# Four query heads of the second batch loaded ahead of its second keys and values, and the last batch's first expert layer in eight block products instead of seven

## The chip, the cores and the metric

The kernel runs on one core of one Trainium2 chip. The metric is the device time of one execution in microseconds (us). Three executions of the kernel before took 369.51, 369.53 and 370.15 us, median 369.53 us. A difference of about 0.2% (0.74 us) is the least that a measurement of this kernel can tell from no change.

Five engines work side by side, each on its own queue in order: PE (TensorE, matrix products, with PEld for its weight loads), DVE (VectorE), ACT (ScalarE), POOL (GpSimd) and SP (SyncE, which here only issues transfers). Sixteen DMA engines move data. PE reads from SBUF and writes to PSUM.

## The reference

Attention over sorted blocks, then a mixture of four experts. Sizes: batch 4, 8 heads, 768 positions, head size 64; 8 blocks of 96 positions.

```
P = sort_net                      # (4, 8, 8, 8)
repeat 5 times:
    P = exp(P - max); P = P / rowsum; P = P / colsum
k_sorted[b,h,i] = sum_j P[b,h,i,j] k_block[b,h,j]      # v the same
attn = softmax(q_block k_sorted_block^T / 8)           # 96 x 96, block by block
x = attn v_sorted_block                                # (4*768, 512)
p = domain_probs / sum(domain_probs)                   # (3072, 4)
out = sum_e p[:, e] * (relu(x w1[e]) w2[e])            # w1 512x1024, w2 1024x512
```

All products are computed on PE with 16-bit operands and sums of 32 bits.

## The kernel before, in words

**Batches and chunks.** The expert layers of a batch are done in three chunks of 256 tokens. While PE computes the experts of batch b, the attention of batch b+1 is worked in between: the lists `PLAN0` (for b = 0) and `PLAN` (b = 1, 2) name, for each chunk and each slot in it, which attention step is called there. A slot is a place between groups of matmuls. The order of instructions on each engine is the order in which the Python code issues them. The chunks of batch 0 do expert 0 ahead, in functions of their own.

**Attention steps of a batch.** Per pair of heads `pr` (0 to 3): `st_v` and `st_k` mix the blocks of values and keys on PE, ACT copies the result; `st_q` transposes the queries of the pair by a DMA on SP's queue (tile `qT`); `st_s` makes the scores on PE (line 405) from `kT` and `qT`; `st_a` makes attn times v (line 437), DVE normalises it into `xsl`; `st_x` transposes `xsl` into the expert input `xT` by a DMA on SP's queue. Keys, values and queries come from memory by DMAs on POOL's queue (`load_natural`, line 109, four heads at a time; `load_queries`, line 120, one head at a time; `st_n` loads the two heads of one pair). They lie in slices of one tile, `arena`. Each load on POOL's queue also waits for the eighth load before it to have landed.

**Start of batch 1's attention.** After the last expert weights (27 to 38 us of landing time each) POOL's queue has, in this order: values 0, keys 0, query heads 0 and 1, values 1, keys 1 (the numbers are the halves of the heads), then three additions of the first chunk's output, then query heads 2 and 3, two additions, query heads 4 to 7. Heads 2 and 3 stand in slot 11 of chunk 0 of `PLAN0`, heads 4, 5 and 6, 7 in slots 0 and 4 of chunk 1.

**First expert layer of a chunk, batches 1 and 2** (`chunk_first`): for each of four experts two groups of 16 matmuls, each with 128x128 weights and 256 columns of `xT` (line 742), into a PSUM buffer of two banks (`psM`, two buffers). DVE then takes max with zero times the token's expert weight from PSUM into `Hb` (line 748) and makes sums of `Hb` blocks into `Sb` (`h_sums`, lines 725 to 731). `pb`, the token weights of a chunk, is loaded on SP's queue once the last user of the chunk before it is done.

**Second expert layer, all chunks:** seven block products instead of eight (a two by two block scheme with sums of blocks), each of 16 matmuls of 256 columns (line 777; line 1069 in the last batch), with the sums of `w2` blocks made once on DVE. DVE, ACT and POOL add up the results, SP stores them.

**Last batch before the change** (`last_chunk`, `seven`): the first layer, too, is done in seven block products per expert. The weight sums s1 to s3 lie in `arena`, s4 in place of a block of `w1`; `input_sums` makes these 16 sums on DVE (line 919) during batch 2, by the list `PLAN_A`. `token_sums` makes four sums of `xT` blocks per chunk (line 935). Each product is 8 matmuls with 128x128 weights and 128 columns (line 981), so 56 per expert and chunk. Partial sums are chained in PSUM banks X, Z, Q; ACT and DVE copy and add them (lines 1001, 1008, 1016, 1017, 1025), and the results go into `Hb` by DVE (line 987) and by ACT with POOL (lines 993, 994). `last_banks` takes over the PSUM of the other pools and issues one matmul of 512 columns (line 948) twice. The first matmul of the next chunk's product, and the product p6 of expert 0, stand inside the last product of the chunk before.

Of the kernel before, what the change touches and what calls it, by code (L numbers as in the profile page):

```python
# [9 lines left out]
F32 = mybir.dt.float32  # L10
# [7 lines left out]
def kernel(  # L18
# [38 lines left out]

    openM, openA = [ctx.enter_context(ExitStack()) for _ in range(2)]
    psM = openM.enter_context(tc.tile_pool(name="psM", bufs=2, space=bass.MemoryType.PSUM))
    psA = openA.enter_context(tc.tile_pool(name="psA", bufs=2, space=bass.MemoryType.PSUM, side="right"))  # L60
# [36 lines left out]

    NW = 4 * R * D
    NQ = NPB * R * 2 * D
    arena = const.tile([P, 4 * NW + NQ + 4 * 4 * P + R * 4 * VW], F16, name="arena")  # L100

# [3 lines left out]
    def load_natural(b, nm, qd):  # L105
        src = {"k": k, "v": v}[nm]
        t = arena[:, ds(("k", "v").index(nm) * 2 * NW + qd * NW, NW)].rearrange("p (h r d) -> p h r d", h=4, r=R)
        natural[(b, nm, qd)] = t
        nc.gpsimd.dma_start(
            t.rearrange("p h r d -> p h (r d)"),  # L110
            src[b, ds(4 * qd, 4)].rearrange("h (p r) d -> p h (r d)", r=R),
        )

    def load_queries(b, heads=range(H)):

        if (b, "q") not in natural:
            natural[(b, "q")] = arena[:, ds(4 * NW, NQ)].rearrange("p (n t h d) -> p n t h d", n=NPB, t=R, h=2)
        t = natural[(b, "q")]
        for h in heads:
            nc.gpsimd.dma_start(t[:, h // 2, :, h % 2, :], q[b, h].rearrange("(t p) d -> p t d", p=P))  # L120
# [64 lines left out]
    kTs, ETs, vs0s, wide = [], [], [], []  # L185
# [4 lines left out]
    for n in range(4):  # L190
        ET = const.tile([P, S + 32], F16, name=f"ET_{n}")
        nc.gpsimd.memset(ET[0:BLK, ds(S, 32)], 0.0)
        ETs.append(ET[0:BLK])
        wide.append(ET)
# [4 lines left out]
    vo = arena[:, ds(4 * NW + NQ + 4 * 4 * P, R * 4 * VW)].rearrange("p (r h w) -> p r h w", r=R, h=4)  # L199
# [122 lines left out]
    def build_PI(eng, n, which):  # L322
        r4 = Rs[:, ds(4 * n, 4), :]
        if which == "k":
            PIk[n] = arena[:, ds(4 * NW + NQ + n % 2 * 4 * P, 4 * P)].rearrange("p (g i c) -> p g i c", g=4, i=NB)
# [6 lines left out]
        else:  # L332
            PIv[n] = arena[:, ds(4 * NW + NQ + (2 + n % 2) * 4 * P, 4 * P)].rearrange("p (g c i) -> p g c i", g=4, i=NB)
# [15 lines left out]
    def st_v(b, pr):  # L349
# [13 lines left out]
        if pr % 2:  # L363
            qd = pr // 2
            vs = att.tile([P, NB, 4, VW], F16, name=f"vs_{b}_{qd}", tag="vs")[0:BLK]
# [63 lines left out]
    def st_a(b, pr):  # L429
        xsl = att.tile([P, NB, 2, D], F16, name=f"xsl_{b}_{pr}", tag="xsl")[0:BLK]  # L430
# [109 lines left out]
    def h_a(qd, qq, ps=None):  # L540
# [11 lines left out]
        if qq not in xsls0:  # L552
            xsls0[qq] = att.tile([P, 2, 4, 2, D], F16, name=f"xsl0_{qq}", tag="xsl")[0:BLK]
# [38 lines left out]
    def stage(b, f, pr):  # L592
# [20 lines left out]
        (0, 9, st_v, 0), (0, 10, st_q, 0), (0, 10, st_v, 1), (0, 11, st_k, 0), (0, 11, st_n, 1), (1, 0, st_q, 1),  # L613
        (1, 0, st_s, 0), (1, 0, st_n, 2), (1, 1, st_k, 1), (1, 1, st_v, 2), (1, 2, st_v, 3), (1, 3, st_q, 2),
        (1, 4, st_s, 1), (1, 4, st_n, 3), (1, 5, st_a, 0), (1, 6, st_x, 0), (1, 7, st_k, 2), (1, 7, st_lv, 0),
# [141 lines left out]
    def chunk(b, c, slot, done=()):  # L757
# [7 lines left out]
        nxt = (b, c + 1) if c + 1 < R // 2 else (b + 1, 0)  # L765
        pbs[nxt] = load_p(*nxt)
# [4 lines left out]
        def product(n, lhs, rhs, pool=psm):  # L771
            ps = pool([P, DH], F32, f"ps_{n}_{b}_{c}")
            for e in es:
                if pool is last_bank and e == 2:
                    last["e0"][6]()
# [15 lines left out]
        if b:  # L791
# [5 lines left out]
            slot()  # L797
            nc.scalar.copy(p5[:], product("p5", sm(0), "t1"))
# [11 lines left out]
            tt(oa2, product("p3", sm(3), "b22", last_bank if last else psm), oa2, ALU.add)  # L810
            slot()
            nc.sync.dma_start(o[:, 2 * c, :], oa[:])
# [24 lines left out]
        def last_adds(u3):  # L837
            gtt(ob2, u3, ob2, ALU.add)
            tt(ob1, ob1, u3, ALU.add)
# [4 lines left out]
        if c == 0:  # L844
# [21 lines left out]
            last_adds(u3[:])  # L866
            f4()
            store(1, ob)
        else:
# [18 lines left out]
            last_adds(u3[:])  # L888
# [4 lines left out]

    AW = 2 * KH * P

    def a_block(n):
        return arena[:, ds(n * AW, AW)].rearrange("p (k f) -> p k f", k=2)  # L900


    A_ORDER = (3, 4, 5, 10, 11, 0, 1, 2, 6, 7, 8, 9)
    As = []
    for e in range(E):
        w, hk, hf = w1sb[e], NKC // 2, FF // 2
        As.append({
            "a11": w[:, 0:hk, 0:hf], "a12": w[:, hk:NKC, 0:hf],
            "a21": w[:, 0:hk, hf:FF], "a22": w[:, hk:NKC, hf:FF], "s4": w[:, 0:hk, hf:FF],
            "s1": a_block(A_ORDER[3 * e]), "s3": a_block(A_ORDER[3 * e + 1]), "s2": a_block(A_ORDER[3 * e + 2]),  # L910
        })

    def input_sums(e, n):
        a = As[e]
        dst, x, y, op = (
            ("s1", "a21", "a22", ALU.add), ("s3", "a11", "a21", ALU.subtract),
            ("s2", "s1", "a11", ALU.subtract), ("s4", "a12", "s2", ALU.subtract),
        )[n]
        nc.vector.tensor_tensor(a[dst], a[x], a[y], op)

    Bs = {}

    def token_sums(c):

        b = B - 1
        xT = xTs[b].rearrange("p k i x -> p k (i x)")
        blk = lambda k, t: xT[:, ds(2 * k, 2), ds((2 * c + t) * P, P)]
        t3 = kTs[c % 2][:, 0:3 * 2 * P].rearrange("p (n k x) -> p n k x", n=3, k=2)
        t = Bs[c] = {
            "b11": blk(0, 0), "b12": blk(0, 1), "b21": blk(1, 0), "b22": blk(1, 1),  # L930
            "t1": t3[:, 0], "t2": t3[:, 1], "t3": t3[:, 2],
            "t4": wide[c % 2][:, 0:2 * P].rearrange("p (k x) -> p k x", k=2),
        }
        for dst, x, y in (("t1", "b12", "b11"), ("t2", "b22", "t1"), ("t3", "b22", "b12"), ("t4", "b21", "t2")):
            nc.vector.tensor_tensor(t[dst], t[x], t[y], ALU.subtract)

    last = {}

    def last_banks(n):

        (openA, openM)[n].close()
        pool = ctx.enter_context(tc.tile_pool(name=f"ps7_{n}", bufs=1, space=bass.MemoryType.PSUM, side=("right", "left")[n]))
        for nm, m in (("X", 1), ("Z", 1), ("Q", 2)):
            last[nm] = last.get(nm, []) + [
                pool.tile([P, 512], F32, tag=f"{nm}{i}", name=f"ps_{nm}{n}{i}") for i in range(m)
            ]

        nc.tensor.matmul(last["X"][n][:], w1sb[0][:, 0, 0:P], w1sb[0][:, 1, 0:512], start=True, stop=True)

    def prepare_last():  # L950

        last_banks(0)
        last["n"] = 1
        t = moe.tile([P, NKC, NB, BLK], F16, name="tmp7", tag="xT").rearrange("p k i x -> p (k i x)").bitcast(F32)
        room = [t[:, ds(n * 512, 512)] for n in range(3)]
        for m in range(2):
            t = att.tile([P, NB, 4, VW], F16, name=f"tmp7_{m}", tag="vs").rearrange("p i h w -> p (i h w)")
            t = t[:, 0:2048].bitcast(F32)
            room += [t[:, 0:512], t[:, 512:1024]]
        t = att.tile([P, NB, 2, D], F16, name="tmp7_2", tag="xsl").rearrange("p i h d -> p (i h d)").bitcast(F32)  # L960
        room.append(t)
        for n, nm in enumerate(("u2", "u3", "t22", "t12")):
            last[nm] = room[2 * n:2 * n + 2]

    def last_bank(shape, dtype, name):
        n = last["n"]
        last["n"] += 1
        return last["Q"][2 - n % 2][:, 0:shape[1]]

    def seven(c, e):  # L970

        b = B - 1
        a, t, pb = As[e], Bs[c], pbs[(b, c)]
        X, Z, u2, u3, t22, t12 = [last[nm][e % 2] for nm in ("X", "Z", "u2", "u3", "t22", "t12")]
        X, Z, Q = X[:], Z[:], last["Q"][e][:]
        tt = nc.vector.tensor_tensor

        def product(dst, lhs, rhs, first=False):
            for f in range(KH):
                for k in range(2):  # L980
                    nc.tensor.matmul(  # L981
                        dst[:, ds(f * P, P)], a[lhs][:, k, ds(f * P, P)], t[rhs][:, k, :],
                        start=(first and f == 0 and k == 0), stop=(f == KH - 1 and k == 1), skip_group_check=True,
                    )

        def finish(i, j, src):
            nc.vector.scalar_tensor_tensor(
                out=Hb[:, e, ds(i * KH, KH), ds(j * P, P)], in0=src.rearrange("p (f x) -> p f x", f=KH), scalar=0.0,
                op0=ALU.max, in1=pb[:, ds(e, 1), ds(j * P, P)].broadcast_to([P, KH, P]), op1=ALU.mult,
            )  # L990

        def finish2(i, j, src):
            nc.scalar.activation(src, src, AF.Relu, bias=0.0, scale=1.0)  # L993
            nc.gpsimd.tensor_tensor(  # L994
# [8 lines left out]
        def p5():  # L1003
            product(Q, "s1", "t1", True)
# [291 lines left out]
```

## Time and profile before

| | |
|---|---|
| profiled execution, its own time | 369.51 us |
| its span (first to last instruction) | 367.7 us |
| outside the span | 1.81 us |
| median of three executions | 369.53 us |
| PE busy | 358.5 us, 97% of the span, 4229 matmuls |
| DVE busy | 277.5 us, 75% |
| ACT, POOL busy | 121.5 us, 118.6 us |
| first-layer products of the last batch (line 981) | 672 matmuls of 128 columns, 287.0 to 353.8 us |
| last matmul starts its group of 16 at | 362.48 us |

The page gives busy time per engine, a clock row of TensorE, and groups of instructions by line. A matmul's duration runs from its start to the modelled end of its result, so that neighbours overlap; what a stream of them costs is read from start to start: the start of the next group minus the start of this one, over the count. In a timeline row the columns are start, duration, engine, line, operation, written tile and read tiles, shapes, count; a bracket at the end gives the idle time before it and what ended that.

### The profile page before, as it was taken

To read this page: it belongs to the slowest core of one execution; us is meant where nothing else is said; L and a number is where in the kernel's file an instruction comes from. 1 tells how busy PE (TensorE), PEld (TensorE's weight loads), DVE (VectorE), ACT (ScalarE), POOL (GpSimd) and SP (SyncE) were. 2 spreads that over 40 slices of the span, in tenths; PEclk is the share of its full clock that TensorE was granted. 3 is DMA by queue.
4 is the path that set the end of the run, shared out by engine and by line. 5 is a ranking of instruction groups with operands and counts; after the bars stand their busy time and mean duration, and the time that the engine had idled before them with its cause. 6 is when DMAs were issued, how large, how long until landed. Compare 5 with 4: busy or idle time off the path is not lost.

```text
span 367.7 us, 9859 instructions
## 1 busy us (share of the span) xinstructions
PE 358.5 (97%) x4229; PEld 313.8 (85%) x4229; DVE 277.5 (75%) x521; ACT 121.5 (33%) x217; POOL 118.6 (32%) x146
## 2 busy tenths in 40 slices
PE   8799999999999999999999999999999999999996
PEld 8685858879889888898898888998888998998985
DVE  5654898766888774696695685698899879789695
ACT  2664330444230334222100235322011381561740
POOL 8872101713836403000921000100200283282471
PEclk9999999999999999999999999999999999999999
DMA  8999999996996768832795223604204102102101
GB/s 115 207 207 230 209 209 198 199 167 101 175 191 133 107 96 106 170 59 66 109 58 79 87 61 64 152 10 80 78 2 81 58 3 59 59 2 60 60 17 43
DMA packets 69752, 38.31 MB, mean 104 GB/s; under 512 B 40390, under 2 KB 64716, under 8 KB 69708
## 3 DMA queue, kind: packets, MB, share of 16 engines
q0 software_dynamic: 34640, 17.83, 37.3%
q1 hardware_dynamic: 35068, 19.85, 26.8%
q8 instruction: 33, 0.54, 0.6%
q14 instruction: 11, 0.09, 0.1%
HBM read 42.00 MB, written 6.34 MB: 131 GB/s over the span
## 4 chain that ended last, share of the span: by engine, by line
PE 80%; DMA 11%; DVE 5%; POOL 1%; issue 1%; ACT 1%; DVEq 0%; ACTq 0%
PE ps_h L742 28%; PE ps_p L777 23%; PE ps_Q L1069 8%; PE ps_X L981 4%; DMA w<-in_moe_w_dram 4%; DMA xT<-xsl 3%; PE ps_Q L981 3%; PE ps_Z L981 3%; PE ps_o L682 3%; DMA qT<-arena 2%; DMA arena<-in_q_dram 2%; PE ps_h L647 1%; PE ps_s L405 1%; DVE Sb L725 1%; PE ps_a L437 1%
## 5 line engine op out<-in xcount | busy, mean ns | idle before, releaser
L742 PE MATMUL ps_h<-xT,w 128*128 128x256 f16 x1056 | 121.0, 273 | 0.0
L742 PEld LDWEIGHTS <-w 128*128 128x128 f16 x1056 | 102.1, 98 | 13.1
L748 DVE SCALAR_TENSOR_TENSOR Hb<-ps_h,pb 128x1024 f16<-128x1024 f32 x66 | 80.7, 1223 | 29.5 <-PE ps_h L742 29.0
L777 PEld LDWEIGHTS <-Sb 128*128 128x128 f16 x528 | 50.9, 98 | 6.9 <-issue 0.3
L777 PEld LDWEIGHTS <-Hb 128*128 128x128 f16 x396 | 38.1, 98 | 4.6
L804 POOL TENSOR_TENSOR oa<-u,p 128x256 f32<-128x256 f32 x6 | 4.9, 809 | 103.9 <-issue 89.1
L994 POOL TENSOR_TENSOR Hb<-tmp,pb 128x512 f16<-128x512 f32 x24 | 30.9, 1293 | 20.2 <-ACT tmp L993 19.0
L395 ACT CAST kT<-ps_k 64x384 f16<-64x384 f32 x48 | 22.7, 473 | 38.2 <-PE ps_k L386 37.3
L412 ACT ACTIVATE ET<-ps_s 96x768 f16<-96x768 f32 x24 | 18.0, 802 | 46.2 <-PE ps_s L405 46.2
L777 PE MATMUL ps_p<-w,Hb 128*128 128x256 f16 x264 | 31.6, 273 | 0.0
L777 PE MATMUL ps_p<-T,Sb 128*128 128x256 f16 x264 | 31.1, 273 | 0.0
L777 PE MATMUL ps_p<-w,Sb 128*128 128x256 f16 x248 | 29.9, 273 | 0.1
L120 POOL DMA_DIRECT2D arena<-in_q_dram x24 | 19.9, 853 | 12.1 <-DMA w<-in_moe_w_dram 9.7
L981 PEld LDWEIGHTS <-w 128*128 128x128 f16 x384 | 23.3, 98 | 0.4
L725 DVE TENSOR_TENSOR Sb<-Hb 128x512 f16<-128x512 f16 x45 | 22.5, 511 | 0.0
L1069 PEld LDWEIGHTS <-Sb 128*128 128x128 f16 x192 | 18.3, 98 | 3.4 <-issue 0.9
L727 DVE TENSOR_TENSOR Sb<-Sb,Hb 128x512 f16<-128x512 f16 x45 | 18.3, 416 | 0.4
L729 DVE TENSOR_TENSOR Sb<-Hb 128x512 f16<-128x512 f16 x45 | 18.1, 418 | 0.0
L422 DVE TENSOR_TENSOR xsl<-ps_a,rz 96x512 f16<-96x512 f32 x24 | 16.5, 687 | 1.4 <-DMA xT<-xsl 0.6
L981 PEld LDWEIGHTS <-arena 128*128 128x128 f16 x288 | 17.4, 98 | 0.1
L731 DVE TENSOR_TENSOR Sb<-Hb,Sb 128x512 f16<-128x512 f16 x45 | 16.6, 425 | 0.0
L993 ACT ACTIVATE tmp<-tmp 128x512 f32<-128x512 f32 x24 | 15.2, 635 | 3.2 <-DVE tmp L1025 2.6
(173 smaller groups left out, 514.9 us busy)
## 6 DMA issues: line engine op xcount, KB each, us to landing
w<-in_moe_w_dram POOLq DMA_DIRECT2D x7, 1024.0 KB, 27.0
pb<-p_dram SPq DMA_DIRECT2D x12, 512.0 KB, 5.1
arena<-in_k_dram POOLq DMA_DIRECT2D x8, 384.0 KB, 7.9
arena<-in_v_dram POOLq DMA_DIRECT2D x8, 384.0 KB, 8.8
vs<-arena SPq DMA_DIRECT2D x36, 66.0 KB, 4.5
arena<-in_q_dram POOLq DMA_DIRECT2D x24, 96.0 KB, 6.5
out_dram<-ob SPq DMA_DIRECT2D x9, 256.0 KB, 2.2
out_dram<-oa SPq DMA_DIRECT2D x8, 256.0 KB, 2.3
```

The lines of the kernel that those rows point to most:

```text
L120: nc.gpsimd.dma_start(t[:, h // 2, :, h % 2, :], q[b, h].rearrange("(t p) d -> p t d", p=P))
L395: nc.scalar.copy(kT[ds(D * hh, D), r], pk[ds(D * r, D), hh].rearrange("p a (i c) -> p a i c", c=CP),)
L412: nc.scalar.activation(ETs[2 * (pr % 2) + hh][:, 0:S].rearrange("c (a x) -> c a x", a=2), pss[hh][0:BLK, :, 0:HS], AF.Exp, bias=0.0, scale ...
L725: tt(sm[0], blk(0, 1), blk(1, 1), ALU.add)
L727: tt(sm[1], sm[0], blk(0, 0), ALU.subtract)
L729: tt(sm[2], blk(0, 0), blk(0, 1), ALU.subtract)
L742: nc.tensor.matmul(ps[:, f, :], w1sb[e][:, kc, ds((4 * g + f) * P, P)], xT[:, kc, ds(2 * c * P, 2 * P)], start=(kc == 0), stop=(kc == NKC ...
L748: nc.vector.scalar_tensor_tensor(out=Hb[:, e, ds(4 * g, 4), :], in0=ps[:], scalar=0.0, op0=ALU.max, in1=pb[:, ds(e, 1), :].broadcast_to([P ...
L777: nc.tensor.matmul(ps[:], lhs(e, f), Ts[e][rhs][:, f, :], start=(e == es[0] and f == 0), stop=(e == E - 1 and f == KH - 1),)
L981: nc.tensor.matmul(dst[:, ds(f * P, P)], a[lhs][:, k, ds(f * P, P)], t[rhs][:, k, :], start=(first and f == 0 and k == 0), stop=(f == KH - ...
L994: nc.gpsimd.tensor_tensor(Hb[:, e, ds(i * KH, KH), ds(j * P, P)], src.rearrange("p (f x) -> p f x", f=KH), pb[:, ds(e, 1), ds(j * P, P)].b ...
L1069: nc.tensor.matmul(ps, lhs(e, f), Ts[e][rhs][:, f, :], start=(e == 0 and f == 0), stop=(e == E - 1 and f == KH - 1),)
```

## The change

The last batch is computed by `chunk`, as the batches before it: `last_chunk`, `seven`, `input_sums`, `token_sums`, `last_banks`, `prepare_last`, `PLAN_A` and the `arena` are gone, and with them the 672 matmuls of 128 columns, for which 384 of 256 columns stand. In the very last chunk the output of the first token block is stored in two halves, as before. Keys, values and queries lie in tiles of a pool `nat` again (two buffers for keys, two for values, one for queries), the mixing matrices in the pool `att`; the buffers are as many as the slices were, but the query tile is now one unit: the first query load of a batch waits for all four transpositions of the batch before, where each slice waited for its own.

The loads of batch 1's keys and values move up in the code, with heads 0 to 3 of the queries between the first half and the second. On POOL's queue this gives: values 0, keys 0, query heads 0, 1, 2, 3, values 1, keys 1, and heads 4 to 7 after the five additions, as before. So heads 2 and 3 pass values 1, keys 1 and three additions. By the rule of the eighth load before, query heads 2 and 3 now wait for two weight loads that values 1 and keys 1 waited for (landed 44.83 and 49.89 us in the profile before), and values 1 and keys 1 wait for the last two weight loads (landed 54.91 and 59.95 us).

```diff
-    openM, openA = [ctx.enter_context(ExitStack()) for _ in range(2)]
-    psM = openM.enter_context(tc.tile_pool(name="psM", bufs=2, space=bass.MemoryType.PSUM))
-    psA = openA.enter_context(tc.tile_pool(name="psA", bufs=2, space=bass.MemoryType.PSUM, side="right"))
+    psA = ctx.enter_context(tc.tile_pool(name="psA", bufs=2, space=bass.MemoryType.PSUM))
+    psM = ctx.enter_context(tc.tile_pool(name="psM", bufs=2, space=bass.MemoryType.PSUM))
+    nat = ctx.enter_context(tc.tile_pool(name="nat", bufs=2))
...
-        t = arena[:, ds(("k", "v").index(nm) * 2 * NW + qd * NW, NW)].rearrange("p (h r d) -> p h r d", h=4, r=R)
+        t = nat.tile([P, 4, R, D], F16, name=f"nat_{nm}_{b}_{qd}", tag=f"nat_{nm}")
...
-            natural[(b, "q")] = arena[:, ds(4 * NW, NQ)].rearrange("p (n t h d) -> p n t h d", n=NPB, t=R, h=2)
+            natural[(b, "q")] = nat.tile([P, NPB, R, 2, D], F16, name=f"natq_{b}", tag="natq", bufs=1)
...
-        (0, 9, st_v, 0), (0, 10, st_q, 0), (0, 10, st_v, 1), (0, 11, st_k, 0), (0, 11, st_n, 1), (1, 0, st_q, 1),
-        (1, 0, st_s, 0), (1, 0, st_n, 2), (1, 1, st_k, 1), (1, 1, st_v, 2), (1, 2, st_v, 3), (1, 3, st_q, 2),
-        (1, 4, st_s, 1), (1, 4, st_n, 3), (1, 5, st_a, 0), (1, 6, st_x, 0), (1, 7, st_k, 2), (1, 7, st_lv, 0),
+        (0, 9, st_v, 0), (0, 10, st_q, 0), (0, 10, st_v, 1), (0, 11, st_k, 0), (0, 12, st_n, 2), (1, 0, st_q, 1),
+        (1, 0, st_s, 0), (1, 0, st_n, 3), (1, 1, st_k, 1), (1, 1, st_v, 2), (1, 2, st_v, 3), (1, 3, st_q, 2),
+        (1, 4, st_s, 1), (1, 5, st_a, 0), (1, 6, st_x, 0), (1, 7, st_k, 2), (1, 7, st_lv, 0),
...
-                if pool is last_bank and e == 2:
-                    last["e0"][6]()
...
+            parts = 2 if (b, c) == (B - 1, R // 2 - 1) else 1
+            if parts == 2:
+                nc.sync.dma_start(o[:, 2 * c, 0:DH], oa1)
...
-    def input_sums(e, n):
...
-    def token_sums(c):
...
-    def last_banks(n):
...
-    def seven(c, e):
...
-    def last_chunk(c):
...
-    PLAN_A = [
...
     builds(1)
+    for qd in range(2):
+        for nm in ("v", "k"):
+            load_natural(1, nm, qd)
+        if qd == 0:
+            load_queries(1, range(4))
...
     second_layer0(0, next_stages)
-    for qd in range(2):
-        for nm in ("v", "k"):
-            load_natural(1, nm, qd)
-        if qd == 0:
-            load_queries(1, range(2))
...
-        if b == B - 1:
-            for c in range(R // 2):
-                last_chunk(c)
-            break
...
-                if b == B - 2:
-                    for cc, n, e, m in PLAN_A:
-                        if (cc, n) == (c, at[0]):
-                            input_sums(e, m)
...
```

## The prediction

> **What bounds the kernel now.** I read the page first, then busy time by stretch, then the order in time on PE, then the queues of SP and POOL.
>
> ```profile
> span 367.7 us, 9859 instructions
> PE 358.5 (97%) x4229; PEld 313.8 (85%) x4229; DVE 277.5 (75%) x521; ACT 121.5 (33%) x217; POOL 118.6 (32%) x146
> PEclk9999999999999999999999999999999999999999
> ```
>
> PE is busy 97% of the span at the full clock in every slice; no other engine is near. So PE's work and PE's holes are the whole account. The stretches (length, busy time and count of each engine) show where the holes are:
>
> ```profile
> 0.00:28.00 28.00, 24.39 (x534) 22.27 (x534) 16.29 (x53) 14.95 (x28) 22.54 (x46) 1.00 1.11 177
> 28.00:60.50 32.50, 32.06 (x335) 21.63 (x330) 23.65 (x39) 10.63 (x14) 4.69 (x6) 1.00 1.20 214
> 60.50:88.00 27.50, 26.54 (x281) 22.77 (x279) 20.30 (x32) 10.96 (x19) 10.24 (x13) 1.00 1.45 168
> 88.00:117.70 29.70, 29.23 (x329) 25.70 (x327) 25.42 (x52) 7.91 (x15) 16.80 (x21) 1.00 1.24 161
> 175.74:202.98 27.24, 27.24 (x274) 24.25 (x272) 19.36 (x34) 2.62 (x5) 11.99 (x14) 1.00 0.73 83
> 287.00:312.31 25.31, 25.21 (x340) 23.48 (x337) 21.21 (x43) 12.36 (x23) 12.06 (x11) 1.00 0.14 43
> ```
>
> After 28 us PE lacks 0.44, 0.96 and 0.47 us in the three stretches of batch 0. A chunk of batch 1 (175.74 to 202.98) has no hole, and one of the last batch (287.00 to 312.31) 0.1. So what the last batch costs is matmuls times spacing, read from start to start. A chunk with the plain first layer, then pieces of the last batch:
>
> ```profile
> 175.74 5.40 PE L742 MATMUL ps_h<-xT,w 128*128 128x256 f16 x48
> 181.08 0.51 PE L405 MATMUL ps_s<-qT,kT 64*128 64x96 f16 x16
> 181.52 8.91 PE L742 MATMUL ps_h<-xT,w 128*128 128x256 f16 x80
> 190.27 1.91 PE L777 MATMUL ps_p<-w,Hb 128*128 128x256 f16 x16
> 192.01 0.65 PE L437 MATMUL ps_a<-vs,ET 96*128 96x65 f16 x16
> 192.50 1.91 PE L777 MATMUL ps_p<-T,Hb 128*128 128x256 f16 x16
> ```
> ```profile
> 291.20 0.61 PE L981 MATMUL ps_X<-kT,arena 128*128 128x128 f16 x8
> 291.65 0.61 PE L981 MATMUL ps_Q<-kT,arena 128*128 128x128 f16 x8
> ...
> 305.01 1.91 PE L1069 MATMUL ps_Q<-T,Hb 128*128 128x256 f16 x16
> 307.02 1.95 PE L1069 MATMUL ps_Q<-w,Sb 128*128 128x256 f16 x16
> ```
>
> 80 matmuls of 256 columns take 190.27 - 181.52 = 8.75 us, 0.1093 us each. 8 of 128 columns take about 0.447 us (291.20 to 291.65, and 20 such steps from 291.20 to 300.13), 0.0559 us each: half the columns, half the time.
>
> The hole that the query loads touch, on PE and on SP's queue:
>
> ```profile
> 82.19 0.51 PE L405 MATMUL ps_s<-qT,kT 64*128 64x96 f16 x16 [0.85 <-DMA qT<-arena]
> ```
> ```profile
> 65.19 1.31 SPq L374 DMA_TRANSPOSE qT<-arena  x1
> 68.88 3.89 SPq L367 DMA_DIRECT2D vs<-arena  x6
> 72.86 1.08 SPq L842 DMA_DIRECT2D out_dram<-oacc  x2
> 75.06 2.39 SPq L374 DMA_TRANSPOSE qT<-arena  x1
> ```
>
> The scores of pair 1 stood 0.85 us for its transposed queries. That transposition was issued at 75.06, just when heads 2 and 3 had landed (issued on POOL's queue from 68.30, the second landing 75.04).
>
> **The change, part by part.**
>
> *1. First layer of the last batch.* Out: 12 times (three chunks, four experts) 56 x 0.0559 = 3.130 us. In: 12 times 32 x 0.1093 = 3.498 us. Sum +4.4 us, on PE, which has no hole to hide it.
>
> The Trainium skill, page "TensorE: Matmul & The Clock Gate", section "Back-to-back issue gap", speaks against this step: it gives about 81 ns per matmul for a sustained stream of weight load and matmul pairs at 128 columns. By that figure (an estimate) seven products would cost 56 x 0.081 = 4.54 us, and the change would save 12.5 us; the rows here are such a stream of pairs and show 55.9 ns, so the measurement decides.
>
> *2. What goes with the seven products.* Two matmuls of 512 columns (line 948): the next group follows 0.21 us after each, -0.42 us. Three waits for the first `Sb` sums: the product p4 of a chunk ends its issue at 305.01 + 16 x 0.1093 = 306.76, p5 starts at 307.02; the other two chunks show 0.30 (330.06 + 1.75 to 332.11) and 0.31 (355.14 + 1.75 to 357.20): -0.87 us. In the plain chunk these sums are made between the groups of the first layer; in batch 1's chunk p5 followed p2 without a gap. The 16 weight sums on DVE (16 x 0.68 = 10.9 us) all lie in batch 2, where PE shows full stretches; they cost PE only in its last chunk, where the 80 matmuls took 8.91 us from start to start against 8.75: -0.16 us. ACT (12.36 us busy per chunk of the last batch) and POOL are relieved too, which gains nothing: neither ends a wait of PE there.
>
> Parts 1 and 2: +2.95 us. A check by whole chunks: batch 1's chunk, 27.24, less its scores 0.44 and its attn-times-v 0.49, is 26.3 us; 240 x 0.1093 is 26.2. Batch 2's last chunk started at 261.14; 27.24 for it and three of 26.3 end at 367.3, three of 26.2 at 367.0. Before, the last product's issue ended at 362.48 + 1.75 = 364.23. That is +2.8 to +3.1; I keep +2.95.
>
> *3. Does DVE keep up without the attention pieces?* Per expert PE takes 3.50 us. DVE started the same step of successive experts in batch 1 at 185.29 and 188.78, 3.49 apart, at most 0.28 us behind PE, with two PSUM buffers between them. If it fell behind by the sum of the durations (2 x 1.22 + 3 x 0.42 = 3.70) it would lag 0.2 us an expert, at most 0.3 us of stall per chunk. I take 0, because the batch 1 row ran 80 matmuls at full spacing with this very sequence; bounds 0 to +0.9 us.
>
> *4. Heads 2 and 3 earlier.* On POOL they follow weight loads landed at 44.83 and 49.89, so they are issued near 45.4 and 50.2 where values 1 and keys 1 stood. They land right behind heads 0 and 1 (64.44 and 65.13), one step of 0.69 each, near 66.5 instead of 75.04. The transposition of pair 1 then waits for its place in SP's queue only, behind six `vs` copies and two stores, near 74.0; with the same 7.1 us to landing it is there at 81.1, and PE would want it at 82.19 - 0.85 = 81.34. The stall goes: -0.85 us. What is late next: values 1 and keys 1 now wait for weights landed at 54.91 and 59.95 and for two query heads, 1.4 us; before they landed at 67.83 and 71.05, so now near 69.2 and 72.4. First uses on PE are at 75.15 (values) and 87.50 (keys): hidden, with 6 us of cover for the values. Behind keys 1 in POOL's queue stands an addition that starts at 62.31; keys 1 is issued by 60.8, so nothing moves. Heads 4 to 7 keep their place after the five additions; two of these start without 1.7 us of query issue before them, but they wait for DVE until 69.75 anyway.
>
> The other cover is thinner. The token weights `pb` (landed 70.93, wanted by DVE at 72.72) and the transposition of pair 0 (landed 71.75, wanted by PE at 72.61) share the DMA engines with these loads. If both slip by the full 1.4 us, PE stalls 71.75 + 1.4 - 72.61 = 0.5 us for pair 0, and `pb` is still in time. If the two queues share evenly, about half, and nothing is late. I take +0.1.
>
> The one query tile makes batch 2's first query load wait for the last transposition of batch 1 (landed 99.93) instead of starting at 96.77: 3.2 us of POOL, eight issues of 0.85, done near 107.6 with keys behind; POOL's next addition starts at 109.94 after ACT. Hidden. The hole at 100.04 (0.47 us, `xsl` waiting for a transposition) has the same queue before it and stays. Bounds of part 4: -1.32 (both holes gone) to +0.5 (first stall stays in another form, second not gained); taken -0.75.
>
> **Sum.** +4.4 - 0.42 - 0.87 - 0.16 - 0.75 = +2.2 us. The span goes from 367.7 to 369.9, the profiled execution from 369.51 to 371.7; it stands 0.02 us under the median of the three runs, so the forecast is 371.7 us, 0.6% slower.
>
> **Rivals.**
> *A. The query loads do not pay.* Pair 1's transposition stays late behind the stores, or pair 0's becomes late. For it: all 16 DMA engines are busy in this stretch (DMA share 1.45 in the row above, over two queues), and a `pb` load takes 9.1 us there against 5.1 as a median. Against: two loads less at 68 to 75 us, where the stores and pair 1 stand. +2.95 with 0 to +0.5: 372.5 to 373.0 us.
> *B. DVE becomes the bound in the last batch*, because no attention gives it room: part 3's +0.9: 372.6 us, with A 373.9. Against: the 8.75 us row.
> *C. Not slower: the plain matmuls run at the pace of their weight loads.* The mean weight load lasts 98 ns. If 256 columns could be spaced at 98 ns, part 1 would be zero and the sum -2.2 us: 367.3 us. It decides the sign once the spacing is under 0.1093 - 2.2/384 = 0.1036 us. Against: every group at line 742 and line 777 shows 0.109.
> *D. More holes close:* all of 0.96 and 0.47 us in batch 0: +2.95 - 1.43 = 371.0 us. Still slower.
>
> **How the numbers follow.** The difference that can be measured is 0.2%, 0.74 us: faster means below 368.8, slower above 370.3. Forecast (371.2 to 372.2) 0.66, A 0.16, B 0.08, D 0.06, C 0.04. A to 373.0 and D to 370.9, with the 0.2 us between the two chunk counts taken off below, give 370.7 to 373.0; outside it are C, half of B and little of D, some 0.15 with what I did not think of. Cases A, B, D and the forecast are slower: 0.94; C is split with no change: 0.03 and 0.03.
>
> **What would show it.** Right: first-layer groups of 32 matmuls 3.49 us apart in the last batch, its three chunks 26.2 to 26.3 us each; no gap before p5; no idle at the scores of pair 1; heads 2 and 3 landing near 66.5. Wrong: idle on PE for `Hb` or PSUM in the last batch (B), a wait of the scores for `qT` near 72 or 81 us (A), a spacing under 0.104 us (C).

## The result, and the profile after

The changed kernel took 374.16 us (median of 373.47, 373.89, 374.43 and 375.04) against 369.52 us before, a ratio of 1.0125 with a 95% interval of 1.0099 to 1.0152. It is slower, as forecast, but by 4.64 us instead of 2.2, and outside the range of 370.7 to 373.0. Run again beside other kernels (f1 below) it took 373.71 us against 370.09, a ratio of 1.0085 (1.0059 to 1.0110). Times are medians; the ratios and their intervals are estimated from the executions as a whole, so a ratio need not be the quotient of the two medians beside it.

The profiled execution is the slowest of the four, 375.04 us with a span of 373.3 us. From the page and the waits of PE (us in total, times, longest):

```profile
span 373.3 us, 9075 instructions
PE 362.2 (97%) x3939; PEld 314.3 (84%) x3939; DVE 259.0 (69%) x469; ACT 87.8 (24%) x157; POOL 86.2 (23%) x122
PEclk9999999999999999999999999999999999999999
```
```profile
PE ps_s L398 <- DMA qT<-natq: 2.5, 2, 1.4
PE ps_R L297 <- DVE sn L285: 1.1, 1, 1.1
PE ps_w L241 <- DVE Hb L141: 1.1, 1, 1.1
PE ps_h L640 <- DMA w<-in_moe_w_dram: 1.0, 1, 1.0
PE ps_mv L467 <- DMA nat_v<-in_v_dram: 1.0, 1, 1.0
```

PE is still 97% busy at full clock. The wait for the transposed queries, 0.85 us once before, is now 2.5 us in two pieces. The waits for the first weights and values are of the start-up, before any load that was moved.

The last batch on PE, and its three chunks as stretches (length, busy time and count of PE, PEld, DVE, ACT, POOL, then clock, DMA share, GB/s; ahead of the chunks the stretches from 60.5 to 117.7 us). The DMA share is the time that packets took over that of 16 engines; with packets of two queues under way at once it can pass 1.

```profile
291.12 14.14 PE L735 MATMUL ps_h<-xT,w 128*128 128x256 f16 x128
305.09 1.91 PE L769 MATMUL ps_p<-w,Hb 128*128 128x256 f16 x16
306.84 1.91 PE L769 MATMUL ps_p<-T,Hb 128*128 128x256 f16 x16
308.58 1.91 PE L769 MATMUL ps_p<-w,Hb 128*128 128x256 f16 x16
310.33 1.91 PE L769 MATMUL ps_p<-w,Sb 128*128 128x256 f16 x16
312.08 3.66 PE L769 MATMUL ps_p<-T,Sb 128*128 128x256 f16 x32
315.57 1.91 PE L769 MATMUL ps_p<-w,Sb 128*128 128x256 f16 x16
317.32 14.14 PE L735 MATMUL ps_h<-xT,w 128*128 128x256 f16 x128
```
```profile
60.50:88.00 27.50, 24.88 (x262) 21.26 (x260) 17.42 (x27) 10.60 (x18) 8.43 (x10) 1.00 1.51 162
88.00:117.70 29.70, 29.52 (x336) 25.98 (x333) 25.97 (x53) 8.29 (x16) 15.13 (x19) 1.00 1.34 166
291.12:317.32 26.20, 26.20 (x243) 23.48 (x240) 17.73 (x30) 1.12 (x3) 1.45 (x2) 1.00 0.14 42
317.32:343.52 26.20, 26.20 (x243) 23.49 (x240) 17.75 (x30) 1.12 (x3) 1.45 (x2) 1.00 0.12 41
343.52:369.72 26.20, 26.20 (x242) 23.39 (x239) 17.74 (x30) 1.12 (x3) 1.45 (x2) 1.00 0.07 26
```

128 first-layer matmuls take 305.09 - 291.12 = 13.97 us, 0.1091 each, without a hole, and every chunk is 26.20 us. So the last batch went as worked out. The stretch from 60.5 to 88 us lacks 2.62 us of PE where it lacked 0.96 before.

A comparison that leaves the start-up out: the second traced execution of the changed kernel (f1) and the traced one before both start the first group at full speed of batch 0's first chunk at 56.9 us (56.88 and 56.85). The scores of pair 0 and pair 1 on PE, before and then f1:

```profile
72.61 0.52 PE L405 MATMUL ps_s<-qT,kT 64*128 64x96 f16 x16
82.19 0.51 PE L405 MATMUL ps_s<-qT,kT 64*128 64x96 f16 x16 [0.85 <-DMA qT<-arena]
```
```profile
74.17 0.52 PE L398 MATMUL ps_s<-qT,kT 64*128 64x96 f16 x16 [1.47 <-DMA qT<-natq]
83.99 0.51 PE L398 MATMUL ps_s<-qT,kT 64*128 64x96 f16 x16 [1.08 <-DMA qT<-natq]
```

and SP's queue of f1:

```profile
61.83 0.38 SPq L205 DMA_DIRECT2D pb<-p_dram  x1
65.66 1.31 SPq L367 DMA_TRANSPOSE qT<-natq  x1
68.90 3.89 SPq L360 DMA_DIRECT2D vs<-vo  x6
72.89 1.58 SPq L841 DMA_DIRECT2D out_dram<-oacc  x2
74.83 1.40 SPq L367 DMA_TRANSPOSE qT<-natq  x1
```

Pair 0, which had not waited before, waits 1.47 us, and pair 1 waits 1.08 instead of 0.85, though its transposition was issued a little sooner (74.83 against 75.06). The last scores on PE (pair 3 of batch 3) start at 268.13 in f1 and at 266.48 before, +1.65 us; from there to the end of the span it is 104.05 us against 101.23, +2.82 us.

### The profile page after: what moved, and what is told of

Same layout as the page of the kernel before. It is cut to its first block, busy times and chain, and to the rows that moved or that the text cites. A ratio compares the mean times of both kernels' runs of the same rounds, so it can differ in the third digit from the quotient of the medians.

```text
span 373.3 us, 9075 instructions
## 1 busy us (share of the span) xinstructions
PE 362.2 (97%) x3939; PEld 314.3 (84%) x3939; DVE 259.0 (69%) x469; ACT 87.8 (24%) x157; POOL 86.2 (23%) x122
## 4 chain that ended last, share of the span: by engine, by line
PE 82%; DMA 12%; DVE 3%; ACT 1%; POOL 1%; issue 0%; DVEq 0%; SPq 0%; ACTq 0%
PE ps_h L735 39%; PE ps_p L769 34%; DMA w<-in_moe_w_dram 4%; DMA xT<-xsl 3%; PE ps_o L675 3%; DMA qT<-natq 2%; DMA vs<-vo 2%; PE ps_h L640 1%; PE ps_s L398 1%; PE ps_a L430 1%; PE ps_v L346 1%; PE ps_k L379 1%; DVE xsl L415 1%; DMA sn<-in_sort_net_dram 0%; POOL sn L285 0%
## 5 line engine op out<-in xcount | busy, mean ns | idle before, releaser
L735 PE MATMUL ps_h<-xT,w 128*128 128x256 f16 x1440 | 163.3, 273 | 0.0
L735 PEld LDWEIGHTS <-w 128*128 128x128 f16 x1440 | 139.7, 98 | 17.3
L741 DVE SCALAR_TENSOR_TENSOR Hb<-ps_h,pb 128x1024 f16<-128x1024 f32 x90 | 110.1, 1223 | 41.9 <-PE ps_h L735 40.3
L769 PEld LDWEIGHTS <-Hb 128*128 128x128 f16 x540 | 52.2, 98 | 6.1
L769 PE MATMUL ps_p<-w,Sb 128*128 128x256 f16 x360 | 43.3, 273 | 0.1
L769 PE MATMUL ps_p<-w,Hb 128*128 128x256 f16 x360 | 43.1, 272 | 0.0
L769 PE MATMUL ps_p<-T,Sb 128*128 128x256 f16 x360 | 42.1, 273 | 0.0
L114 POOL DMA_DIRECT2D natq<-in_q_dram x24 | 19.8, 849 | 22.0 <-DMA w<-in_moe_w_dram 18.4
L769 PE MATMUL ps_p<-T,Hb 128*128 128x256 f16 x180 | 21.6, 272 | 0.0
L352 ACT CAST vo<-ps_v 128x768 f16<-128x768 f32 x12 | 9.5, 802 | 19.3 <-PE ps_v L346 19.3
```

Source lines behind the costliest of these rows:

```text
L735: nc.tensor.matmul(ps[:, f, :], w1sb[e][:, kc, ds((4 * g + f) * P, P)], xT[:, kc, ds(2 * c * P, 2 * P)], start=(kc == 0), stop=(kc == NKC ...
L741: nc.vector.scalar_tensor_tensor(out=Hb[:, e, ds(4 * g, 4), :], in0=ps[:], scalar=0.0, op0=ALU.max, in1=pb[:, ds(e, 1), :].broadcast_to([P ...
L769: nc.tensor.matmul(ps[:], lhs(e, f), Ts[e][rhs][:, f, :], start=(e == es[0] and f == 0), stop=(e == E - 1 and f == KH - 1),)
```

## The experiments

The question after the result was where the rest comes from: the plain last batch, the order of the query loads, or the start-up. The table has one traced execution of every kernel but e2, us from its start. "Weights" is when the last expert weights landed, "pair 0" and "pair 1" when those transpositions landed (their issue plus the time to landing), the last column the time from the last scores on PE to the end.

| kernel | weights | pair 0 | after weights | PE idle | pair 1 | PE idle | last scores to end |
|---|---|---|---|---|---|---|---|
| before | 59.95 | 71.75 | 11.8 | 0 | 82.14 | 0.85 | 101.23 |
| after | 61.71 | 75.31 | 13.6 | 1.45 | 85.20 | 1.06 | 104.05 |
| f1, after again | 60.42 | 74.03 | 13.6 | 1.47 | 83.94 | 1.08 | 104.05 |
| e1, plain last batch only | 60.02 | 72.10 | 12.1 | 0.43 | 82.68 | 1.75 | 104.03 |
| f2, query loads only | 60.32 | 73.93 | 13.6 | 1.45 | 83.43 | 0.68 | 101.22 |
| f4, after without heads 2, 3 | 59.95 | 72.34 | 12.4 | 0.22 | 82.73 | 1.57 | 104.00 |
| e3, after, heads 2, 3 behind | 59.73 | 72.79 | 13.1 | 0.97 | 81.46 | 0 | 104.03 |
| e4, after, keys 1 last | 60.31 | 71.69 | 11.4 | 0 | 85.34 | 4.66 | 104.04 |
| g3, after, pair 1 ahead of stores | 60.56 | 74.17 | 13.6 | 1.86 | 80.42 | 0 | 104.05 |
| f3, before, both moved | 59.90 | 72.86 | 13.0 | 1.17 | 80.28 | 0 | 101.24 |
| g1, before, pair 1 ahead of stores | 60.22 | 72.42 | 12.2 | 0.14 | 80.62 | 0 | 101.19 |
| g2, g1 and `pb` behind pair 0 | 61.20 | 71.67 | 10.5 | 0 | 82.36 | 0.01 | 101.21 |
| g4, g1 and scores later | 61.13 | 73.06 | 11.9 | 0 | 81.11 | 0 | 101.23 |

**e1: the plain last batch alone.** The changed kernel with loads and plan put back:

```diff
-    for qd in range(2):
-        for nm in ("v", "k"):
-            load_natural(1, nm, qd)
-        if qd == 0:
-            load_queries(1, range(4))
...
     second_layer0(0, next_stages)
+    for qd in range(2):
+        for nm in ("v", "k"):
+            load_natural(1, nm, qd)
+        if qd == 0:
+            load_queries(1, range(2))
...
-        (0, 11, st_k, 0), (0, 12, st_n, 2), (1, 0, st_q, 1),
+        (0, 11, st_k, 0), (0, 11, st_n, 1), (1, 0, st_q, 1),
```

> The changed kernel with the query loads and the plan of slots put back as they were, so that only the plain last batch (and the tiles in pools) is left. Theory 'two terms' (plain last batch +2.75 us, query loads about +1.35 us, the rest start-up that differs from execution to execution): 372.3 us, no idle at the scores of pair 0, 0.85 us at those of pair 1. Rival 'start-up' (the pools' place in memory delays the first weights and values by 1.3 us in every execution): 373.6 us, first chunk group of the first batch (32 matmuls) starting near 58.2 us instead of 56.9.

Measured: 373.02 us (372.24 to 375.42), ratio to before 1.0103 (1.0075 to 1.0130). Every traced execution of a plain last batch needs 104.0 us from the last scores to the end, every one in seven products 101.2. This term is +2.8 us and does not vary. The start-up rival, a delay by the pools in every execution, falls: the first chunk of batch 0 starts at 55.98 us here and at 56.88 in f1, with the same pools, so the 58.17 of the first trace was that execution. Pair 1's idle was 1.75 us with the old order, so that 0.85 was also one execution's value; and pair 0 waited too, where none was expected:

```profile
72.23 0.52 PE L398 MATMUL ps_s<-qT,kT 64*128 64x96 f16 x16 [0.43 <-DMA qT<-natq]
82.72 0.52 PE L398 MATMUL ps_s<-qT,kT 64*128 64x96 f16 x16 [1.75 <-DMA qT<-natq]
```

**e2: the query loads alone, first try.** The kernel before, the loads moved up in the code as the change has them:

```diff
     builds(1)
+    for qd in range(2):
+        for nm in ("v", "k"):
+            load_natural(1, nm, qd)
+        if qd == 0:
+            load_queries(1, range(4))
```

> The kernel before with the order of loads and the plan of slots of the changed kernel, the last batch in seven products. Theory 'two terms': 370.9 us, idle of about 1.45 us at the scores of pair 0 and of about 1.0 at those of pair 1. The prediction's working: 368.8 us, no idle at either. Rival 'start-up': as the kernel before in its first 57 us.

Measured: 405.81 us, and nothing on the question. In `arena` the slices keep no old contents, so loads that stand ahead of batch 0's readers in the code come first: batch 0 computes from batch 1's values and keys and waits for them, and its first chunk starts at 75.97 us. With tiles from a pool, as in the change, the loads wait for batch 0's readers wherever they stand. f2 does what this was for.

**e3: heads 2 and 3 behind values 1 and keys 1.**

```diff
         if qd == 0:
-            load_queries(1, range(4))
+            load_queries(1, range(2))
+    load_queries(1, range(2, 4))
```

> The changed kernel with query heads 2 and 3 loaded behind values 1 and keys 1, still ahead of the three additions. Theory 'place in the queue' (heads 2 and 3 cost because they stand ahead of values 1 and keys 1, which then run beside the transposition of pair 0): that transposition lands within 0.5 us of where it did before, idle there 0 to 0.4 us, time 372.8 us. Theory 'all work counts' (the DMA engines are full and serve every queue in turn, so all that is issued ahead of the transposition delays it): idle there 1.0 to 1.5 us, time as the changed kernel, 374.2 us.

Measured: 372.38 us (371.11 to 374.97), 1.0083 (1.0053 to 1.0112). Idle at pair 0 0.97 us, between the two theories: behind values 1 and keys 1 the two heads cost pair 0 some 0.5 us less than ahead of them, but not nothing. So both the place and the amount count. Pair 1 has no wait in this trace, though its transposition still stands behind the two stores: it landed 7.4 us after its issue (74.04 to 81.46).

**e4: keys 1 behind query heads 4 to 7.**

```diff
+    def st_k1(b, qd):
+        load_natural(b, "k", qd)
...
-        (1, 0, st_n, 3),
+        (1, 0, st_n, 3), (1, 0, st_k1, 1),
```

> The changed kernel with keys 1 loaded behind query heads 4 to 7, some 384 KB less ahead of the transposition of pair 0. Both theories of the queue: no idle at the scores of pair 0 (-1.45 us). 'All work counts': keys 1 then delay the transposition of pair 1 instead, idle there 1.5 to 2.5 us, time 373.3 to 374.2 us. 'Place in the queue': idle there at most 1.0 us, time 372.7 us.

Measured: 374.79 us, its six executions in two groups (371.72 to 373.06 and 376.51 to 377.40), and the traced one, the longest of them, ran at a clock of 0.991. That trace has no idle at pair 0, as both theories say, and 4.66 us at pair 1, over what either theory gave. One execution of this kind decides nothing on pair 1, and with such a spread there is no verdict on the time.

**f1: the changed kernel again**, no edit.

> The changed kernel once more, beside the next three on one chip. From the first traces: stretch from the start to the scores of pair 3 for batch 3 about 266 to 269 us (it differs from execution to execution), from there to the end 104.0 us in every execution. 374 us, idle at the scores of pair 0 of 1 us or more.

Measured: 373.71 us (373.12 to 374.37). Idle 1.47 us at pair 0, again 13.6 us after the last weights.

**f2: the query loads alone.** The kernel before, the loads left where they stand in the code:

```diff
         if qd == 0:
-            load_queries(1, range(2))
+            load_queries(1, range(4))
...
-        (0, 11, st_k, 0), (0, 11, st_n, 1), (1, 0, st_q, 1),
+        (0, 11, st_k, 0), (0, 12, st_n, 2), (1, 0, st_q, 1),
```

> The kernel before with query heads 2 and 3 ahead of values 1 and keys 1 and the plan of slots of the changed kernel; nothing else. Theory 'two races' (the DMA engines work without a break until about 80 us; loads put ahead of the transposition of pair 0 delay it by their own time, 1.7 us or more, past PE's arrival): idle at the scores of pair 0 of 1.0 to 1.8 us, time 370.5 to 371.2 us. The prediction's working: no idle at pair 1, at most 0.1 us at pair 0, 368.8 us.

Measured: 370.34 us against 370.09, ratio 1.0010 (0.9994 to 1.0026): between -0.2 and +1.0 us. The two scores on PE:

```profile
74.07 0.52 PE L405 MATMUL ps_s<-qT,kT 64*128 64x96 f16 x16 [1.45 <-DMA qT<-arena]
83.48 0.51 PE L405 MATMUL ps_s<-qT,kT 64*128 64x96 f16 x16 [0.68 <-DMA qT<-arena]
```

The wait at pair 0 came with the loads, as "two races" said, and the wait at pair 1 stayed. The gain of 0.85 us did not come: the interval excludes the -0.75 us of the prediction's part 4. The median rose 0.25 us, less than the 0.4 to 1.1 us expected; the interval excludes neither that nor no change. Between the two traces the last scores come 0.73 us later (267.21 against 266.48), and a wait of 0.47 us at 100 us is gone.

**f4: the changed kernel without heads 2 and 3 of batch 1**, a constant in their place:

```diff
         if qd == 0:
-            load_queries(1, range(4))
+            load_queries(1, range(2))
+            nc.gpsimd.memset(natural[(1, "q")][:, 1], 0.1)
```

> The changed kernel without the loads of query heads 2 and 3 of the second batch: a constant written on POOL stands in their place, so these heads' attention is computed from other numbers. Takes the suspected cost away and leaves the order. Theory 'two races': the transposition of pair 0 lands 1.7 us or more earlier against the last weights, idle there 0 to 0.5 us, 372.4 to 373.0 us. Rival 'start-up or pools': as the changed kernel, 374 us.

Measured: 372.37 us (371.31 to 373.11), 1.34 us under f1. On PE:

```profile
72.47 0.52 PE L398 MATMUL ps_s<-qT,kT 64*128 64x96 f16 x16 [0.22 <-DMA qT<-natq]
82.78 0.52 PE L398 MATMUL ps_s<-qT,kT 64*128 64x96 f16 x16 [1.57 <-DMA qT<-natq]
```

With 192 KB of loads gone pair 0 lands 12.4 us after the last weights instead of 13.6, and its wait falls from 1.47 to 0.22 us. So these two loads are what made pair 0 late here. (f4 leaves the loads out; it does not put them back behind, so its 1.34 us is not the cost of their order.) Pair 1 waits 1.57 us though its two heads are not loaded at all: its wait is not one for heads 2 and 3.

**f3 and g1: pair 1's transposition ahead of the stores.** g1 is the kernel before with

```diff
-        (0, 11, st_k, 0), (0, 11, st_n, 1), (1, 0, st_q, 1),
+        (0, 11, st_k, 0), (0, 11, st_n, 1), (0, 11, st_q, 1),
```

f3 has it too, and heads 2 and 3 behind keys 1 as in e3.

> The kernel before with query heads 2 and 3 behind values 1 and keys 1, and with the transposition of pair 1 issued ahead of the two output stores of the first chunk (512 KB) instead of behind them. Theory 'two races': the stores wait for nobody and nobody for them, so pair 1 lands some 3 us earlier, no idle at its scores; idle at pair 0 stays between 0 and 1 us; time 368.5 to 369.6 us. Rival (the DMA engines' total work sets when pair 1 lands, whatever stands ahead of it): idle at pair 1 as before, 0.8 us, time 369.5 to 370.5 us.

> The kernel before with one change: the transposition of pair 1 is issued ahead of the two output stores of the first chunk; the loads stay. Theory 'two races' (512 KB of stores ahead of it cost it about 3 us): it is issued at about 75 us as before, when heads 2 and 3 have landed, and lands near 79 instead of 82; idle at pair 1 0 instead of 0.85, at pair 0 as before (0 to 0.4): 369.2 us. Rival (the DMA engines' total work): lands near 82, 370.1 us as the kernel before.

Measured: f3 369.67 us, 0.9978 (0.9962 to 0.9994); g1 369.17 us, 0.9976 (0.9952 to 1.0001). In both the wait at pair 1 is gone; f3 waits 1.17 us at pair 0. SP's queue of g1, then the wait at 100 us on PE, before and in g1:

```profile
65.48 1.30 SPq L374 DMA_TRANSPOSE qT<-arena  x1
68.62 3.90 SPq L367 DMA_DIRECT2D vs<-arena  x6
75.75 2.48 SPq L374 DMA_TRANSPOSE qT<-arena  x1
78.33 0.99 SPq L842 DMA_DIRECT2D out_dram<-oacc  x2
```
```profile
100.04 0.51 PE L386 MATMUL ps_k<-arena 128*128 128x128 f16 x6 [0.47 <-DVE xsl L422]
99.89 0.51 PE L386 MATMUL ps_k<-arena 128*128 128x128 f16 x6 [1.28 <-DVE xsl L422]
```

Issued at 75.75, as late as before, it landed after 4.9 us (80.62) instead of 7.1: two stores of 256 KB ahead of it in SP's queue were the difference. In this trace nearly all of the gain comes back: the wait at 100 us, 0.47 before, is 1.28 us here, and the last scores start only 0.16 us earlier (266.32 against 266.48). g1's interval reaches one; f3's lies just under it, by 0.2%, which is the least that can be told and comes from one of four versions of the kernel before, so it is a weak sign of a gain. f3 keeps the last batch in seven products.

**g2: the token weights `pb` of chunk 1 behind pair 0** in SP's queue, on top of g1:

```diff
-        pbs[nxt] = load_p(*nxt)
+        if (b, c) != (0, 0):
+            pbs[nxt] = load_p(*nxt)
...
-        (0, 10, st_q, 0),
+        (0, 10, st_q, 0), (0, 10, st_p, 1),
```

> The same, and the token weights of the second chunk (512 KB) behind the transposition of pair 0 instead of ahead of it. If what stands ahead in SP's queue delays pair 0: it lands 2 us or more earlier, near 69.5, no idle there in any execution; the token weights then land near 72, and if that is too late DVE and then PE wait for them, 0.3 to 2 us. Time 368.8 us without that wait, 370.5 us with it. If only POOL's loads delay pair 0: it lands as before, time 369.2 us.

Measured: 369.40 us, 0.9992 (0.9973 to 1.0010), no difference to before. Pair 0 lands 10.5 us after the last weights instead of 12.2, so what stands ahead in SP's queue counts too, but `pb` then lands at 75.31 and PE pays for it:

```profile
76.68 1.91 PE L745 MATMUL ps_h<-xT,w 128*128 128x256 f16 x16 [1.26 <-DVE Hb L751]
```

The wait at 100 us is 1.79 us in this trace.

**g3: the changed kernel with pair 1 ahead of the stores**, the same edit of the plan.

> The changed kernel with the transposition of pair 1 ahead of the two stores. It separates the two waits: idle at pair 0 stays at 1.4 us (heads 2 and 3 still ahead of values 1 and keys 1), idle at pair 1 goes from 1.07 us to 0: 372.7 us against 373.7. If the changed kernel's wait at pair 1 comes from heads 4 to 7 and not from the stores, 0.5 us or more of it stays: 373.2 us.

Measured: 372.52 us (371.73 to 373.16), 1.0071 (1.0051 to 1.0091), against 373.71 for f1 on another chip, whose ratio of 1.0085 is not apart from this one. On PE:

```profile
74.31 0.52 PE L398 MATMUL ps_s<-qT,kT 64*128 64x96 f16 x16 [1.86 <-DMA qT<-natq]
82.97 0.52 PE L398 MATMUL ps_s<-qT,kT 64*128 64x96 f16 x16
```

The two waits are separate: with the stores out of the way pair 1's is gone, while pair 0's, which came with the loads, stays.

**g4: scores of pair 0 one slot later**, on top of g1:

```diff
-        (1, 0, st_s, 0), (1, 0, st_n, 2), (1, 1, st_k, 1),
+        (1, 0, st_n, 2), (1, 1, st_s, 0), (1, 1, st_k, 1),
```

> The kernel before with the transposition of pair 1 ahead of the stores, and the scores of pair 0 one slot (16 matmuls, 1.75 us) later. Theory 'two races': PE then meets neither transposition late, no idle at either in fast or slow start-ups; 368.8 to 369.2 us, 0.3% under the kernel before. Rival: the later scores make the next steps late (keys or attn times v of pair 0, which follow within five slots), and the time stays at 370.1 us.

Measured: 369.63 us, 1.0000 (0.9981 to 1.0019). No wait at either scores, but the next step now meets ACT's exponentials of the later scores:

```profile
76.57 0.49 PE L386 MATMUL ps_k<-arena 128*128 128x128 f16 x6 [0.95 <-ACT ET L412]
```

The rival named it, and the wait only changed its name.

## Why the prediction was wrong

*Sign and larger part: right.* The plain last batch costs what PE's spacing says. Parts 1 and 2 gave +2.95 us; e1 and the six other traces with the plain last batch show +2.8 against the six with seven products, the same in every one. Part 3's choice (DVE keeps up) held: 128 matmuls at 0.1091 us, no wait on `Hb` or PSUM. The waits before p5 are gone, as said. Rivals B and C fall with this.

*What failed: part 4, the query loads, taken as -0.75 us.* Two of its steps are wrong.

First, "one step of 0.69 each" and "half" of it for pair 0: I priced the two query loads at 1.4 us from the distance between the landings of heads 0 and 1, and let pair 0 slip by half of that, since the queues share. In f1 the second of the two landed at 68.72, 3.1 us after head 1 (65.60), and not near 66.5. In all four traces with the heads ahead of values 1 and keys 1 (after, f1, f2, g3) pair 0 landed 13.6 us after the last weights; in the four with the old loads ahead of it (before, e1, g1, g4) it was 11.8 to 12.2. That is 1.4 to 1.8 us of slip, and 1.2 between f4 and f1: about all of the 1.4, not half. The cover of 0.86 us (72.61 - 71.75) was one execution's: in e1 and g1, with the old loads, PE already waited 0.43 and 0.14 us at pair 0. So the slip went into PE's wait, 1.45 to 1.86 us in the four traces.

Not everything slipped. `pb`, just ahead of pair 0 in SP's queue, landed 9.6 to 10.9 us after the last weights in the four traces with the new order and 10.8 to 11.5 in the four with the old. Keys 1, pushed back by the two heads, landed 12.9 us after the last weights instead of 11.1 to 11.6, and pair 0 landed 0.65 to 0.92 us after keys 1 in all eight. The landings fit a transposition that was held up by the load beside it; no run isolates that.

Second, "with the same 7.1 us to landing". Pair 1 was issued a little earlier, as said, but landed 9.1 us after its issue (74.83 to 83.94 in f1). I took the end of a chain, the landing of heads 2 and 3 at 75.04, for the cause of the wait. It was the release of the issue; the time after the issue went in part to the two stores ahead: without them ahead, in g1, it was 2.2 us shorter. g1 and g3 show that moving the stores behind is enough to end the wait, with either order of loads. It is not the only way: in e3 the stores stayed ahead and pair 1 landed in time, so the loads beside it count too, by how much no run tells. Busy time of the DMA engines fits this; f1, then before:

```profile
62.00:64.00 2.00, 2.00 (x21) 1.79 (x19) 1.93 (x4) 0.25 (x1) 0.96 (x1) 1.00 1.97 165
64.00:66.00 2.00, 1.90 (x18) 1.53 (x16) 2.00 (x6) 0.00 (x0) 0.00 (x0) 1.00 2.00 176
72.00:74.00 2.00, 0.70 (x7) 0.38 (x4) 1.23 (x1) 0.00 (x0) 2.00 (x4) 1.00 1.24 119
```
```profile
62.00:64.00 2.00, 2.00 (x21) 1.79 (x19) 1.93 (x4) 0.23 (x1) 0.96 (x1) 1.00 1.86 182
64.00:66.00 2.00, 1.89 (x18) 1.51 (x16) 2.00 (x6) 0.00 (x0) 0.00 (x0) 1.00 1.41 207
72.00:74.00 2.00, 2.00 (x32) 1.59 (x30) 1.46 (x2) 0.78 (x2) 2.00 (x4) 1.00 2.01 162
```

The second last column is the DMA share. The moved loads fill the stretch from 64 to 66 us (2.00 against 1.41), just ahead of pair 0's transposition, and leave a poorer one at 72 to 74 (1.24 against 2.01), as heads 4 to 7 still wait on POOL for the additions (issued from 71.45 us on, 71.34 before). The work was moved to just ahead of pair 0, and the room that it left was not filled at once.

*Rival A* named this mechanism ("pair 1's transposition stays late behind the stores, or pair 0's becomes late"), and both halves came true. Its price for part 4, 0 to +0.5, is what f2 measured (+0.25, -0.2 to +1.0). It had been given 0.16, and with +2.95 for the last batch it reached 373.0, still under the result.

*The other part 4 statements.* Values 1 and keys 1 landed later (70.86 and 73.36 us in f1, against 69.2 and 72.4 worked out) without being missed by their own users on PE, and POOL's additions did not move, as said. The 3.2 us later start of batch 2's queries, from the one query tile, shows no wait of PE in the first trace of the changed kernel; in f1 PE waited 0.27 us for an `xT` transposition at 119.58, which I had as hidden, and no run tells whether the query tile did it.

*What stays open.* 2.8 us of the last batch and 0.25 (-0.2 to +1.0) of the query loads alone make 3.05 us, 372.6 us, which lies inside the range: part 4 accounts for some 1.0 us (0.5 to 1.8) of the 2.4 between forecast and result. f1 shows +3.6 by the medians and +3.1 (+2.2 to +4.1) by the ratio, which agrees; the first result, +4.64 (+3.7 to +5.6), does not quite. Its executions were 0.45 us slower than f1's, and the start-up of the traced one took 1.3 us more; the rest of the 1.6 us over the two terms is not assigned to any cause. Nor do the times alone show what the order of loads costs inside the changed kernel: e1, with the old order, took 373.02 us on one chip, f1 373.71 on another. Whether the pools cost anything beside the two terms could not be told from the spread either: e1 is over before by 3.1 us by the medians and 3.8 (2.8 to 4.8) by the ratio, 2.8 of it the last batch, while its traced execution, its fastest, reaches the last scores at 266.44 us, as the kernel before does (266.48).

## What to carry to other kernels

Price a matmul change from start to start of groups, on both sides: that held to 0.15 us here. Where a chain of waits ends at a load, ask what the transfer that waited for it still has ahead of it in its own queue, and what the moved load pushes back: here the transposition that landed next paid 1.2 to 1.8 us for two loads priced at 1.4. A wait or a margin taken from one execution is one draw: kernels with the same loads waited 0.85 and 1.75 us at pair 1, and the margin of 0.86 us at pair 0 was a wait of 0.43 in another.

## What the runs showed of the hardware that was not expected

Two loads of one query head each, 96 KB in pieces of 128 bytes, put ahead on POOL's queue delayed a transposition on SP's queue by 1.2 to 1.8 us, while the 512 KB load just ahead of it in its own queue (`pb`) did not land later. Two stores of 256 KB ahead in its own queue cost a transposition 2.2 us (7.1 us from issue to landing in the trace before, 4.9 in g1).

The start-up differs between executions: in two traces of the changed kernel (after and f1) batch 0's first chunk began at 58.17 and 56.88 us and the last weights landed at 61.71 and 60.42. A quick start need not be a gain: in e1 it began at 55.98, and PE then waited 2.2 us in all for the two transpositions. From the last scores on, thirteen traces agree within 0.05 us for each form of the last batch.
